# Spilled and kept rows of a branchformer backward kernel: 128-partition transfers in place of 112 and 13, with a new instruction order

## The chip, the cores and the metric

The kernel runs on one core of a Trainium2 chip. The metric is device time in microseconds (us) of one execution; three runs of the kernel before gave 1150.36, 1152.78 and 1153.01 us, so its median is 1152.78 us. Less is better.

## What is computed

Forward and all gradients of one branchformer block, for two batches of 4000 tokens of 144 channels, in bfloat16. Cut to what matters:

```python
B, T, D, K = 2, 4000, 144, 5
xa = layernorm(x)
q, k, v = split(xa @ w_qkv)
p = softmax(q @ k.T * D ** -0.5)            # 4000 x 4000 for each batch
glob = (p @ v) @ w_att_out
u, g = split(gelu(xa @ w_mlp_in)); g = layernorm(g)
gc = sum_i shift(g, i) * dw_csgu[i]         # 5 taps over tokens
loc = (u * gc) @ w_mlp_out
m = concat(glob, loc); m = m + sum_i shift(m, i) * dw_merge[i]
out = x + m @ w_merge
# returned: out, and the gradients of out against x and the seven weights, for grad_out
```

## The kernel before

**Tiles and stages.** The 4000 tokens of a batch stand as 125 partitions of 32 tokens (`PB` = 125, `NB` = 32). So every token tile has 125 rows. The kernel has three stages. The *head* loads x, grad_out and the weights, normalises x and multiplies weight matrices together. The *attention loop* then runs over 64 row blocks (32 of each batch), some 15 us each. The *end* multiplies the outputs and the gradients of the weights.

**The attention loop.** For row block `i` TensorE writes scores and, one step later, the gradient of the probabilities into PSUM (`ps`, two buffers, in runs of eight matmuls; the lines of `quad`). VectorE reads each piece of scores with L1209, which puts the negative into `Pbuf` and keeps its minimum; ScalarE makes exponentials of it in place (L1215) and copies the other half out of PSUM (L1225); VectorE multiplies (L1226). Each half of a row block of `Pbuf` and `Sbuf` is then turned by a transposing DMA on SyncE's queue into `PT` and `ST` (L1219, L1405), and TensorE multiplies those by xa (`yz`, L1236 and L1266) and adds up `X` (L1322), which VectorE adds to `acc` (L1329). `qb` and `dhr` go through transposing DMAs too.

**Beside it** the local branch (`local_units`) runs for pairs of token blocks, in steps 2 to 26 for batch 0 and again for batch 1. Its 16 pairs are visited starting with the last one, because the five taps reach over block borders; what the last pair left in the ring tiles `hgr` (u and the gate), `dugr` and `gpr` (gate values) goes out to DRAM tiles `keep` when it is made (`e_gp`) and comes back into slot 0 near the end (`e_hold`). `held` does the same for two pairs of the taps' ring.

**Spills.** There is no room for both batches, so batch 0's normalised x (`xa_aug`) goes to `xa_d` in eight pieces (`spill_xa0`) and its sums (`acc`, f32) to `acc_d` in four (`spill_acc0`); in the end stage `load_xa0` and `load_acc0` bring them back into `xa0r` and `acc0`.

**How 125 rows travel.** Each such transfer is made by `move` as two DMAs, one of partitions 0 to 111 and one of the last 13 (L47 and L48). `Yn_d`, `Zn_d` and `ug_d` already have 128 rows and go in one DMA each.

**What sets the order.** Each engine's instructions are first written in program order. `Planner.plan` then cuts them into runs (up to 8 or 16 matmuls on TensorE, one instruction elsewhere) and chains the runs of each engine in the order that a table of numbers, `Planner.ORDER`, gives. SyncE's DMAs are one such list, GpSimd's instructions another. An engine takes its instructions strictly in this order, so a DMA whose input is late holds up every DMA behind it on SyncE's queue.

Of the kernel before, what the change touches and what calls it, by code (L numbers as in the profile page):

```python
# [8 lines left out]
BF = mybir.dt.bfloat16  # L9
# [514 lines left out]
def local_units(k, W, b, S, A, es, DHT, ps_w, gw):  # L524
# [11 lines left out]
    keep = [tc.dram_tile([PB, G2, n], BF, name="keep%d_%d" % (b, i)) for i, n in enumerate((D, D, 2 * D))]  # L536
# [12 lines left out]
    hgr = mk("hgr", [PB, G2, 2 * D], 3)  # L549
    dugr = mk("dugr", [PB, G2, D], 3)  # L550
    gpr = mk("gpr", [PB, G2, 2 * D], 3)
# [79 lines left out]
    def e_hold():  # L631
        for i in range(2):
            move(nc.sync, ring[:, :, 8 + 2 * i:10 + 2 * i, :], held[i])
        move(nc.sync, hgr[0][:, :, 0:D], keep[0][:])
        move(nc.sync, dugr[0][:], keep[1][:])
        move(nc.sync, gpr[0][:], keep[2][:])
# [5 lines left out]
    def e_gp(g):  # L642
        nc.vector.tensor_tensor(sq[:], z_[:], a_[:], op=ALU.mult)
        nc.vector.tensor_tensor(gpr[new(g)][:], sq[:], q_[:], op=ALU.add)
        if g == NG2 - 1:
            move(nc.sync, keep[0][:], hgr[new(g)][:, :, 0:D])
            move(nc.sync, keep[1][:], dugr[new(g)][:])
            move(nc.sync, keep[2][:], gpr[new(g)][:])
# [127 lines left out]
class Planner:  # L776

    ORDER = {
# [759 lines left out]
class Merge:  # L1538
# [81 lines left out]
    def open_late(self):  # L1620
# [16 lines left out]
        self.Zn = [None, None]  # L1637
        m0 = self.pool(self.es_m0, "mrg_m0", 1, "left")
        S = self.SS[0]
        S.acc = m0.tile([PB, NB, D], F32, name="acc0")  # L1640
        S.xa_aug = m0.tile([PB, NB, XW], BF, name="xa0r")

    def load_xa0(self):
        k, S = self.k, self.SS[0]
        for g in range(2):
            sl = slice(16 * g, 16 * g + 16)
            move(k.nc.sync, S.xa_aug[:, sl, 0:D], k.xa_d[:, sl, :])
# [545 lines left out]
```

## Time and profile before

| what | value |
|---|---|
| median of 3 runs | 1152.78 us (1150.36 to 1153.01) |
| the profiled execution's own time | 1152.39 us |
| its span, first to last instruction | 1150.5 us |
| TensorE busy | 1118.8 us, 97% |
| VectorE busy | 1021.0 us, 89% |
| ScalarE busy | 906.5 us, 79% |
| GpSimd busy | 249.5 us, 22% |
| SyncE's DMA queue, share of 16 DMA engines' span | 84.6% |

The own time is 1.9 us more than the span: what lies around the first and last instruction. TensorE's busy time is modelled from pipelined matmuls, so a busy TensorE isn't TensorE at its peak. A row of waits names the instruction that waited, what ended the wait, the total in us, the number of waits and the longest. PE is TensorE, PEld its weight loads, DVE VectorE, ACT ScalarE, POOL GpSimd, SP SyncE; a q behind a name is that engine's own queue of issues.

### The profile page before, as it was taken

The numbers are of one execution on the slowest core, as the hardware profiler recorded it, in microseconds if no ns is written. First come the engines' busy times: TensorE is split into PE (matmuls) and PEld (weight loads), VectorE is DVE, ScalarE is ACT, GpSimd is POOL, SyncE is SP. The second block draws the span as 40 slices with busy tenths as digits, with TensorE's granted clock in tenths as the row PEclk, the third lists the DMA queues.
The fourth block names the chain that finished last, engine by engine and source line by source line (L and its number), as shares of the span: only waits on it lengthen the run. The fifth ranks groups of instructions, "written<-read, shape, count | busy, mean of one in ns | idle before, by whom it ended". The sixth has DMA issues, their size and how long they took to land.

```text
span 1150.5 us, 35851 instructions
## 1 busy us (share of the span) xinstructions
PE 1118.8 (97%) x14293; PEld 868.7 (76%) x14293; DVE 1021.0 (89%) x3063; ACT 906.5 (79%) x1641; POOL 249.5 (22%) x427
## 2 busy tenths in 40 slices
PE   6999999999999999999999999999999999999998
PEld 3667777777777677777777777777777777699987
DVE  8699999999999998877999999999999997667656
ACT  5999898899898767777989889888889877615372
POOL 8111112111121113431001111111111112013642
PEclk9999999999999999999999999999999999999999
DMA  4688887979988989998988989888888899978973
GB/s 117 155 160 176 173 181 158 192 159 173 174 166 159 188 181 182 201 187 183 207 183 178 171 158 168 161 181 152 173 174 154 187 177 183 224 173 219 245 144 101
DMA packets 680887, 200.72 MB, mean 174 GB/s; under 512 B 657815, under 2 KB 674093, under 8 KB 680699
## 3 DMA queue, kind: packets, MB, share of 16 engines
q1 hardware_dynamic: 678352, 194.69, 84.6%
q0 software_dynamic: 2192, 3.62, 1.1%
q8 instruction: 111, 1.82, 0.7%
q14 instruction: 56, 0.46, 0.1%
q10 hardware_dynamic: 176, 0.12, 0.0%
HBM read 24.62 MB, written 18.01 MB: 37 GB/s over the span
## 4 chain that ended last, share of the span: by engine, by line
PE 64%; DMA 13%; DVE 11%; ACT 7%; issue 2%; SPq 1%; POOL 1%; ACTq 0%; DVEq 0%; POOLq 0%
PE X L1322 18%; PE ps L1187 14%; PE yz L1236 8%; PE yz L1266 8%; PE ps L1194 5%; DMA PT<-Pbuf 5%; DVE Pbuf L1209 4%; ACT Pbuf L1215 3%; PE po L1708 2%; DMA ST<-Sbuf 2%; PE pd L610 1%; DVE Sbuf L1226 1%; PE pj L1147 1%; ACT Sbuf L1225 1%; DMA go_h<-in_grad_out_dram 1%
## 5 line engine op out<-in xcount | busy, mean ns | idle before, releaser
L1209 DVE TENSOR_SCALAR_CACHE_REDUCE Pbuf<-ps 125x1000 bf16<-125x1000 f32 x256 | 306.2, 1197 | 30.1 <-PE ps L1194 22.4
L1225 ACT CAST Sbuf<-ps 125x1000 bf16<-125x1000 f32 x249 | 248.7, 999 | 86.7 <-PE ps L1194 66.2
L1215 ACT ACTIVATE Pbuf<-Pbuf,nm 125x1000 bf16<-125x1000 bf16 x256 | 284.9, 1144 | 4.4 <-DVE nm L1211 4.2
L1322 PE MATMUL X<-QBs,Pbuf 125*128 125x144 bf16 x2048 | 281.1, 226 | 0.2 <-POOL QBs L1256 0.2
L1322 PE MATMUL X<-QBs,Sbuf 125*128 125x144 bf16 x2048 | 281.3, 226 | 0.0
L1187 PE MATMUL ps<-xaT_m,qt 128*128 128x500 bf16 x1024 | 260.6, 374 | 5.0 <-DVE Pbuf L1209 3.5
L1322 PEld LDWEIGHTS <-Sbuf 125*128 125x128 bf16 x2048 | 198.2, 98 | 18.8 <-issue 18.5
L1322 PEld LDWEIGHTS <-Pbuf 125*128 125x128 bf16 x2048 | 200.2, 98 | 1.3 <-issue 1.1
L1226 DVE TENSOR_TENSOR Sbuf<-Sbuf,Pbuf 125x1024 bf16<-125x1024 bf16 x249 | 170.8, 690 | 7.9 <-ACT Sbuf L1225 6.0
L1236 PE MATMUL yz<-xa_aug,PT 125*128 125x145 bf16 x2048 | 151.0, 227 | 6.5 <-DMA PT<-Pbuf 6.4
L1266 PE MATMUL yz<-xa_aug,ST 125*128 125x144 bf16 x2048 | 150.8, 228 | 3.6 <-DMA ST<-Sbuf 2.4
L1236 PEld LDWEIGHTS <-PT 125*128 125x128 bf16 x2048 | 130.7, 98 | 21.6 <-DMA PT<-Pbuf 10.5
L1187 PEld LDWEIGHTS <-qt 128*128 128x128 bf16 x1024 | 91.4, 97 | 68.6 <-issue 7.0
L1266 PEld LDWEIGHTS <-ST 125*128 125x128 bf16 x2048 | 132.9, 98 | 12.2 <-issue 7.1
L1329 DVE TENSOR_TENSOR acc<-X,acc 125x432 f32<-125x432 f32 (+1 forms) x204 | 109.8, 548 | 15.3 <-PE X L1322 14.8
L1256 POOL TENSOR_TENSOR QBs<-g,g 125x144 bf16<-125x144 f32 x64 | 35.2, 550 | 379.2 <-ACT g L1255 290.9
L1194 PEld LDWEIGHTS <-qt 16*128 16x128 bf16 x1024 | 26.3, 91 | 108.9 <-issue 108.9
L1194 PE MATMUL ps<-XR,qt 16*128 16x500 bf16 x1016 | 100.4, 380 | 0.0
L681 POOL TENSOR_SCALAR l_w<-ring,nc,c 125x144 f32<-125x144 bf16 x64 | 31.8, 504 | 167.0 <-DVE nc L677 122.4
L653 DVE TENSOR_TENSOR l_prod<-ring,Wc 125x720 bf16<-125x720 bf16 x128 | 65.9, 535 | 0.2
L1611 PE MATMUL Hps<-Yg,go_h 125*128 125x144 bf16 x640 | 54.3, 226 | 0.0
L600 POOL TENSOR_TENSOR rsr<-ve,mhalf 125x2 f32<-125x2 f32 x32 | 25.4, 795 | 126.9 <-DVE ve L599 107.4
(540 smaller groups left out, 1946.4 us busy)
## 6 DMA issues: line engine op xcount, KB each, us to landing
Yn_d<-yn SPq DMA_DIRECT2D x64, 36.0 KB
Zn_d<-qb SPq DMA_DIRECT2D x64, 36.0 KB
ug_d<-ugr SPq DMA_DIRECT2D x32, 72.0 KB
Yg<-Yn_d SPq DMA_DIRECT2D x8, 288.0 KB
Yg<-ug_d SPq DMA_DIRECT2D x8, 288.0 KB
Zn<-Zn_d SPq DMA_DIRECT2D x4, 576.0 KB
PT<-Pbuf SPq DMA_TRANSPOSE x128
ST<-Sbuf SPq DMA_TRANSPOSE x128
```

Of the source, the lines that this page charges most:

```text
L653: nc.vector.tensor_tensor(prod[:, bi].rearrange("p a b -> p (a b)"), ring[:, a, p + bi:p + bi + 5, :].rearrange("p a b -> p (a b)"), W.Wc[ ...
L1187: mm = nc.tensor.matmul(pp[r // 2][:, r % 2, 0:CH], QT[i][:, 2 * h, :], bs(i)[0].xaT_m[:, c * CH:(c + 1) * CH], start=True, stop=False)
L1194: nc.tensor.matmul(pp[r // 2][:, r % 2, 0:CH], QT[i][rs, 2 * h + 1, :], xr, start=False, stop=True)
L1209: nc.vector.tensor_scalar(pv(pc(i, c2)), src, -1.0, 3.0e38, op0=ALU.mult, op1=ALU.min, accum_out=NM[i][:, c2:c2 + 1])
L1215: nc.scalar.activation(v, v, ACT.Exp, bias=NM[i][:, 4:5], scale=-1.0)
L1225: nc.scalar.copy(pv(sc(i, c2)), src)
L1226: nc.vector.tensor_tensor(sc(i, c2), sc(i, c2), pc(i, c2), op=ALU.mult)
L1236: nc.tensor.matmul(Yw, PT[0:PB, pos(i, j), :], S.xa_aug[:, j, 0:D + 1], start=(j == 0), stop=(j == NB - 1))
L1266: nc.tensor.matmul(Zw, ST[0:PB, j, :], S.xa_aug[:, j, 0:D], start=(j == 0), stop=(j == NB - 1))
L1322: nc.tensor.matmul(X[:, jj, :], l, r, start=(n_ == 0), stop=(n_ == len(ops) - 1))
L1329: nc.vector.tensor_tensor(av, X[0:PB, 0:nj, :], av, op=ALU.add)
L1611: nc.tensor.matmul(H[0:rows, a // 3, (a % 3) * D:(a % 3 + 1) * D], lhs, self.src[b][h][:, 2 + j, :], start=(n == 0 and a % 3 == 0), stop=( ...
```

## The change

The tiles `hgr`, `dugr`, `gpr`, `acc`, `xa_aug`, `acc0` and `xa0r` and the DRAM tiles `keep`, `acc_d` and `xa_d` get 128 rows; compute uses views of the first 125. Thirty pairs of DMAs become thirty DMAs of 128 partitions: twelve of `keep` (three out and three back in each batch), eight to `xa_d`, four to `acc_d`, four from it and two from `xa_d`. The three rows that nobody writes are cleared: `acc` and the ring buffers by GpSimd memsets (one of 32 x 4608 f32, three small ones in each batch), `xa_aug` by two DMAs of zeros. `held` still goes as 112 and 13. SyncE's list goes from 826 to 798 instructions, GpSimd's from 423 to 430, and all five lists of `ORDER` are new.

```diff
-    keep = [tc.dram_tile([PB, G2, n], BF, name="keep%d_%d" % (b, i)) for i, n in enumerate((D, D, 2 * D))]
+    keep = [tc.dram_tile([128, G2, n], BF, name="keep%d_%d" % (b, i)) for i, n in enumerate((D, D, 2 * D))]
-    hgr = mk("hgr", [PB, G2, 2 * D], 3)
-    dugr = mk("dugr", [PB, G2, D], 3)
-    gpr = mk("gpr", [PB, G2, 2 * D], 3)
+    def whole(name, n):
+        full = mk(name, [128, G2, n], 3)
+        nc.gpsimd.memset(full[2][96:128], 0.0)
+        return full, [t[0:PB] for t in full]
+    hgf, hgr = whole("hgr", 2 * D)
+    dugf, dugr = whole("dugr", D)
+    gpf, gpr = whole("gpr", 2 * D)
...
-        move(nc.sync, hgr[0][:, :, 0:D], keep[0][:])
+        nc.sync.dma_start(hgf[0][:, :, 0:D], keep[0][:])
...
-            move(nc.sync, keep[0][:], hgr[new(g)][:, :, 0:D])
+            nc.sync.dma_start(keep[0][:], hgf[new(g)][:, :, 0:D])
...
     ORDER = {
-        "PE": [36, 37, 38, 39, 40, 41, 0, 1, 42, 2, 3, 4, 5, 43, ...
+        "PE": [36, 37, 38, 39, 40, 41, 0, 42, 1, 2, 3, 4, 5, 6, 43, ...
...
-            move(k.nc.sync, S.xa_aug[:, sl, 0:D], k.xa_d[:, sl, :])
+            k.nc.sync.dma_start(self.xa0[:, sl, 0:D], k.xa_d[:, sl, :])
...
-            move(k.nc.sync, S.acc[:, sl, :], k.acc_d[:, sl, :])
+            k.nc.sync.dma_start(self.acc0[:, sl, :], k.acc_d[:, sl, :])
...
-    k.spill_xa0 = lambda j: move(nc.sync, k.xa_d[:, j:j + 4, :], SS[0].xa_aug[:, j:j + 4, 0:D])
-    k.spill_acc0 = lambda sl: move(nc.sync, k.acc_d[:, sl, :], acc[:, sl, :])
+    k.spill_xa0 = lambda j: nc.sync.dma_start(k.xa_d[:, j:j + 4, :], SS[0].xa_full[:, j:j + 4, 0:D])
+    k.spill_acc0 = lambda sl: nc.sync.dma_start(k.acc_d[:, sl, :], accf[:, sl, :])
...
     def clear_a():
+        nc.gpsimd.memset(accf[96:128], 0.0)
+        for a, n in ((0, 25), (25, 7)):
+            nc.sync.dma_start(SS[0].xa_full[PB:128, a:a + n, :].rearrange("p a b -> p (a b)"), k.zdram[0:128 - PB, 0:n * XW])
```

SyncE's queue where the program begins, before. `Sbuf<-in_x_dram` are the loads of x, `raw` the weights, `dwt` the merge taps, which TensorE turns at L215:

```order
L42 DMA Sbuf<-in_x_dram 112x1152
L2020 DMA zdram<-zt 128x128
L43 DMA Sbuf<-in_x_dram 13x1152
L42 DMA Sbuf<-in_x_dram 112x1152
L154 DMA raw<-in_w_att_out_dram 16x144
L154 DMA raw<-in_w_merge_dram 16x144
L42 DMA go_q_95<-in_grad_out_dram 112x1152
L1118 DMA Sbuf<-zdram 3x4096
L157 DMA dwt<-in_dw_merge_dram 5x288
```

The same queue from its first DMA, after:

```order
L42 DMA Sbuf<-in_x_dram 112x1152
L43 DMA Sbuf<-in_x_dram 13x1152 x3
L157 DMA dwt<-in_dw_merge_dram 5x288
L42 DMA Sbuf<-in_x_dram 112x1152
L153 DMA raw<-in_w_mlp_out_dram 128x144
L2026 DMA zdram<-zt 128x128
L153 DMA raw<-in_w_merge_dram 128x144
```

The load of `dwt` went from the fourteenth DMA of the queue to the fifth.

SyncE's queue where the kept rows of batch 0 come back, before. `PT` and `ST` are the transposes that TensorE waits for:

```order
L48 DMA ring<-held_0_923 13x2x288
L1405 DMA_TRANSPOSE ST<-Sbuf 128x16x128
L1248 DMA Yn_d_69<-yn_133 128x144
L1219 DMA_TRANSPOSE PT<-Pbuf 128x16x128 x2
L48 DMA hgr_934<-keep_0_926 13x2x144
L1165 DMA_TRANSPOSE qt<-qb_128 128x6x128
L691 DMA_TRANSPOSE dhT<-dhr_948 128x6x128
L48 DMA dugr_937<-keep_1_927 13x288
```

The same place, after (the lines of the same statements are 4 higher):

```order
L1409 DMA_TRANSPOSE ST<-Sbuf 128x16x128
L639 DMA dugr_941<-keep_1_930 128x288
L1252 DMA Yn_d_69<-yn_132 128x144
L1409 DMA_TRANSPOSE ST<-Sbuf 128x16x128
L1223 DMA_TRANSPOSE PT<-Pbuf 128x16x128 x2
L48 DMA ring<-held_1_927 13x2x288
L640 DMA gpr_945<-keep_2_931 128x576
L638 DMA hgr_937<-keep_0_929 128x2x144
```

Three returns of one DMA each stand where six stood, later in the row of transposes and closer together.

GpSimd's queue ahead of the first `QBs` (which `X` needs), before:

```order
L402 COPY go_r_96<-go_q_95 125x608
L548 MEMSET ugr_931 32x288
L2023 MEMSET A_dWiT 128x432
L1256 TENSOR_TENSOR QBs<-g_910,g_911 125x144
L1256 TENSOR_TENSOR QBs<-g_1190,g_1191 125x144
```

and after:

```order
L402 COPY go_r_96<-go_q_95 125x608
L282 TENSOR_TENSOR sr_806<-two,cols 128x80 x2
L282 TENSOR_TENSOR sr_834<-two,cols 128x80
L2029 MEMSET acc 32x4608
L1136 MEMSET yn_133 32x144
L1260 TENSOR_TENSOR QBs<-g_913,g_914 125x144
```

The new memset of `acc` stands two rows ahead of the first `QBs`.

On TensorE the two orders are nearly one: of 1385 runs, 785 stand at the same place in both, and none moved by more than 12. On VectorE 464 of 2521 stand at the same place, and half moved by two or less.

More of the change, by code (lines that the diff above doesn't have):

```diff
@@ L633, in e_hold @@
             move(nc.sync, ring[:, :, 8 + 2 * i:10 + 2 * i, :], held[i])
-        move(nc.sync, hgr[0][:, :, 0:D], keep[0][:])
-        move(nc.sync, dugr[0][:], keep[1][:])
-        move(nc.sync, gpr[0][:], keep[2][:])
+        nc.sync.dma_start(hgf[0][:, :, 0:D], keep[0][:])
+        nc.sync.dma_start(dugf[0][:], keep[1][:])
+        nc.sync.dma_start(gpf[0][:], keep[2][:])
     def e_m(g):
@@ L645, in e_gp @@
         if g == NG2 - 1:
-            move(nc.sync, keep[0][:], hgr[new(g)][:, :, 0:D])
-            move(nc.sync, keep[1][:], dugr[new(g)][:])
-            move(nc.sync, keep[2][:], gpr[new(g)][:])
+            nc.sync.dma_start(keep[0][:], hgf[new(g)][:, :, 0:D])
+            nc.sync.dma_start(keep[1][:], dugf[new(g)][:])
+            nc.sync.dma_start(keep[2][:], gpf[new(g)][:])
     def taps(g, a):
@@ L778 @@
     ORDER = {
[53 rows of a table removed]
-        "DVE": [0, 2, 1, 3, 4, 10, 5, 11, 9, 8, 6, 7, 12, 14, 15, 13, 16, 17, 40, 43, 25, 18, 44, 20, 22, 23, 19, 32, 24, 21, 34, 33, 35, 36, 26, 28,
[99 rows of a table removed]
[53 rows of a table added]
+        "DVE": [0, 2, 3, 1, 4, 9, 11, 8, 5, 6, 7, 10, 12, 14, 15, 16, 17, 21, 13, 18, 23, 25, 22, 19, 20, 24, 32, 44, 34, 40, 33, 35, 36, 41, 26, 43,
[99 rows of a table added]
             2476, 2477, 2478, 2479, 2480, 2456, 2428, 2486, 2485, 2481, 2482, 2483, 2487, 2430, 2484, 2488, 2462, 2491, 2489, 2429, 2427, 2492, 2490,
@@ L934 @@
             2509, 2517, 2510, 2511, 2512, 2518, 2519, 2520],
-        "Activation": [1, 0, 4, 5, 2, 3, 7, 6, 8, 9, 10, 13, 29, 32, 14, 15, 11, 33, 16, 17, 18, 12, 37, 35, 34, 19, 20, 21, 24, 22, 23, 31, 27, 26,
[64 rows of a table removed]
-        "Pool": [8, 5, 15, 4, 11, 0, 12, 10, 1, 3, 47, 7, 2, 16, 18, 6, 19, 17, 41, 25, 26, 24, 50, 33, 32, 31, 9, 53, 37, 38, 20, 30, 42, 23, 13,
[44 rows of a table removed]
+        "Activation": [0, 1, 2, 4, 3, 5, 8, 10, 9, 11, 7, 29, 6, 13, 14, 12, 15, 32, 38, 16, 18, 31, 17, 37, 30, 35, 19, 23, 24, 20, 21, 27, 26, 22,
[64 rows of a table added]
+        "Pool": [2, 7, 0, 5, 6, 47, 8, 15, 4, 11, 9, 1, 12, 16, 18, 19, 10, 41, 17, 26, 25, 24, 32, 33, 31, 37, 50, 3, 38, 20, 35, 42, 34, 30, 22,
[44 rows of a table added]
     }
@@ L1639, in open_late @@
         S = self.SS[0]
-        S.acc = m0.tile([PB, NB, D], F32, name="acc0")
-        S.xa_aug = m0.tile([PB, NB, XW], BF, name="xa0r")
+        self.acc0, self.xa0 = m0.tile([128, NB, D], F32, name="acc0"), m0.tile([128, NB, XW], BF, name="xa0r")
+        S.acc, S.xa_aug = self.acc0[0:PB], self.xa0[0:PB]
     def load_xa0(self):
@@ L1970 @@
     bx = pool(ctx, "bx", "left")
-    acc = bx.tile([PB, NB, D], F32, name="acc")
+    accf = bx.tile([128, NB, D], F32, name="acc")
+    acc = accf[0:PB]
     rstd = [bx.tile([PB, NB], F32, name="rstd_x%d" % b) for b in range(B)]
@@ L1979 @@
             setattr(S, nm + "_d", tc.dram_tile([128, NB, D], BF, name="%s_d%d" % (nm, b)))
-    k.acc_d = tc.dram_tile([PB, NB, D], F32, name="acc_d")
-    k.xa_d = tc.dram_tile([PB, NB, D], BF, name="xa_d")
+    k.acc_d = tc.dram_tile([128, NB, D], F32, name="acc_d")
+    k.xa_d = tc.dram_tile([128, NB, D], BF, name="xa_d")
     def open_batch(b, side):
@@ L1985, in open_batch @@
         px = pool(es_x[b], "xa%d" % b, side)
-        S.xa_aug = px.tile([PB, NB, XW], BF, name="xa_aug%d" % b)
+        S.xa_full = px.tile([128, NB, XW], BF, name="xa_aug%d" % b)
+        S.xa_aug = S.xa_full[0:PB]
         pa = pool(es_x[b], "bt%d" % b, side)
```

516 rows, old and new, of the table ORDER are left out of this document.

## The prediction

> **What bounds the kernel now.** I read the page first: its span and its busy times.
>
> ```profile
> span 1150.5 us, 35851 instructions
> PE 1118.8 (97%) x14293; PEld 868.7 (76%) x14293; DVE 1021.0 (89%) x3063; ACT 906.5 (79%) x1641; POOL 249.5 (22%) x427
> ```
>
> TensorE leaves 31.7 us of the span idle. Nothing that only moves transfers can win more than this. The table by stretches of 50 us then says where the other engines stand (columns: stretch, its length, busy time with count of PE, PEld, DVE, ACT and POOL, granted clock, DMA share, GB/s).
>
> ```profile
> 200.00:250.00 50.00, 50.00 (x638) 38.30 (x637) 49.11 (x147) 45.77 (x80) 9.27 (x16) 1.00 0.84 168
> 400.00:450.00 50.00, 46.47 (x601) 34.64 (x599) 45.02 (x139) 32.18 (x54) 11.47 (x19) 1.00 0.93 184
> ```
>
> In a steady stretch of the attention loop TensorE is busy all 50.00 us and VectorE 49.11; the clock is 1.00. Both engines are full there, and neither number changes with the way in which a spill travels. Where batch 0's local branch ends (second row), TensorE has 3.5 us idle. So the question is which of TensorE's waits are for DMAs. The waits of TensorE, and those of its weight loads, in which a late transpose shows first:
>
> ```profile
> PE hps L170 <- DMA raw<-in_w_qkv_dram: 6.3, 1, 6.3
> PE ps L1187 <- DVE Pbuf L1209: 3.5, 12, 0.9
> ...
> PEld L1236 <- DMA PT<-Pbuf: 10.5, 18, 1.3
> PEld L1266 <- DMA ST<-Sbuf: 4.2, 7, 1.5
> PEld L1187 <- DMA qt<-qb: 1.5, 3, 0.7
> ```
>
> The weight loads wait 10.5 + 4.2 + 1.5 = 16.2 us for transposes in the whole program. None of these waits names a kept or spilled row. Such a row can only cost time by standing ahead of a transpose on SyncE's queue, or by taking the DMA engines from it. The same view by the stretches in which kept and spilled rows travel densest, in order 73 to 97 (first row), 364 to 420 (three rows) and 530 to 605 us (two rows):
>
> ```profile
> PEld L1266 <- DMA ST<-Sbuf: 1.0, 1, 1.0
> ...
> PEld L1236 <- DMA PT<-Pbuf: 2.6, 4, 1.1
> PEld L1187 <- DMA qt<-qb: 0.6, 1, 0.6
> PEld L1266 <- DMA ST<-Sbuf: 0.5, 2, 0.3
> ...
> PEld L1236 <- DMA PT<-Pbuf: 1.3, 1, 1.3
> PEld L1266 <- DMA ST<-Sbuf: 0.3, 1, 0.3
> ```
>
> Together 6.3 us in 10 waits. This is the most that the transfers themselves can give back.
>
> **The change part by part.** *Thirty issues fewer.* The issues of 13 rows on SyncE's queue, from the answers on the tiles `keep`, `acc_d` and `xa_d` (durations in ns, least/median/most):
>
> ```profile
> L48 SPq DMA_DIRECT2D keep<-hgr x2: 842/890/938, 79.9 to 583.1; - x2
> L48 SPq DMA_DIRECT2D keep<-dugr x2: 543/546/550, 88.9 to 574.0; - x2
> L48 SPq DMA_DIRECT2D keep<-gpr x2: 427/480/534, 94.7 to 597.5; - x2
> L48 SPq DMA_DIRECT2D hgr<-keep x2: 863/865/867, 378.7 to 908.2; - x2
> L48 SPq DMA_DIRECT2D dugr<-keep x2: 343/415/487, 383.5 to 901.0; - x2
> L48 SPq DMA_DIRECT2D gpr<-keep x2: 389/467/545, 412.3 to 925.3; - x2
> ...
> L48 SPq DMA_DIRECT2D acc_d<-acc x4: 338/460/1199, 536.1 to 589.0; - x4
> L48 SPq DMA_DIRECT2D acc<-acc_d x4: 327/399/403, 1032.9 to 1053.3; - x4
> ...
> L48 SPq DMA_DIRECT2D xa_d<-xa_aug x8: 369/520/547, 27.4 to 510.5; - x8
> L48 SPq DMA_DIRECT2D xa0r<-xa_d x2: 408/980/1553, 1047.2 to 1064.4; - x2
> ```
>
> By medians: `keep` 2 x (0.890 + 0.546 + 0.480 + 0.865 + 0.415 + 0.467) = 7.3 us, `acc_d` 4 x 0.460 + 4 x 0.399 = 3.4, `xa_d` 8 x 0.520 + 2 x 0.980 = 6.1. That is 16.9 us of queue time in 30 issues, 0.56 each, in a span of 1150. All of it is hidden except where a transpose right behind is late. Of the 10 waits I can't say from the trace which has a removed issue ahead of it. If each had one, each would shrink by at most 0.56, and by no more than it is long: below 10 x 0.56 = 5.6 us. The longest of the second stretch (1.1) has none:
>
> ```profile
> 376.85 6.34 DMA PT<-Pbuf
> ...
> 383.23 1.20 PE yz L1236 x16
> ...
> 375.18 3.45 SPq L1219 DMA_TRANSPOSE PT<-Pbuf  x2
> 378.72 0.87 SPq L48 DMA_DIRECT2D hgr<-keep  x1
> ```
>
> Here (the chain, then SyncE's timeline) both transposes were issued ahead of the kept row, and the second took 6.34 us until TensorE could start; what it lost, it lost on the DMA engines. There the change takes no bytes away: 128 rows for 125 are 2.4% more. So I take two fifths of the 6.3 us: **-2.5 us**, between 0 and -5.6.
>
> The Trainium skill (*DMA: Bandwidth & Descriptors*, Rules for kernel authors) says of two transfers to disjoint partition halves that they serialize on the same engines, and to use one of 128 partitions; and that under 64 KB one pays mostly overhead. By that rule the pieces of 13 rows are nearly pure cost, all 5.6 us would come back, and the sum would be 1146.4; the trace agrees that a small piece is no cheaper to issue, and shows no one who waits for it.
>
> *The last rows back in the end stage.* `acc0` has a waiter, on VectorE:
>
> ```profile
>   DVE dx_s L1720: 1.2, 1
> ...
> 1050.00:1100.00 50.00, 49.55 (x805) 49.17 (x802) 36.75 (x165) 20.52 (x39) 31.00 (x52) 1.00 1.00 236
> ```
>
> VectorE has 13 us free in that stretch and TensorE is full, so this 1.2 us costs nothing, and its going gives nothing: 0.
>
> *Clearing.* The memset of 32 x 4608 f32 isn't in the trace. The nearest f32 one:
>
> ```profile
> L2023 POOL MEMSET A_dWiT<- 128x432 f32 x1 | 0.5, 462 | 0.1
> ...
> 42.07 0.33 POOL L548 MEMSET ugr<- 32x288 bf16 x1 [11.26 <-PE pt L350]
> 42.46 0.46 POOL L2023 MEMSET A_dWiT<- 128x432 f32 x1
> 49.48 0.74 POOL L1256 TENSOR_TENSOR QBs<-g,g 125x144 bf16<-125x144 f32 x1 [6.55 <-ACT g L1254]
> ```
>
> 462 ns for 432 elements of a row is 1.07 ns each, so 4608 take some 4.9 us as an estimate. It stands between `go_r` and the first `QBs`, where GpSimd idles 11.26 + 6.55 us. Cost 0; with that cover gone, up to 4.9. The six small ones (288 to 576 elements) are at most 0.6 us each, on an engine that is 22% busy: 0. The two DMAs of zeros go behind the loads of the head, where no transpose is due yet: 0, at worst two issues, 1.1 us.
>
> *The new order at the beginning.* TensorE's transposes of `dwt` waited 1.41 us, since its load was issued as the fourteenth DMA, at 7.43:
>
> ```profile
> 7.43 3.08 DMA dwt<-in_dw_merge_dram
> ...
> 10.56 0.50 PE L215 MATMUL hps<-ident,dwt 5*128 5x5 bf16 x4 [1.41 <-DMA dwt<-in_dw_merge_dram]
> 10.99 0.81 PE L392 MATMUL pt<-ident,xa_aug 125*128 125x125 bf16 x6
> ...
> 9.53 1.05 DVE L385 TENSOR_SCALAR xa_aug<-Sbuf,rstd_x,lnnm 125x144 bf16<-125x144 bf16 x4
> ```
>
> Now it is the fifth, and can land before TensorE gets there. Late next is `xa_aug`: VectorE ends it at 10.58, so L392 starts there instead of 10.99: **-0.4 us**, between 0 and -1.4.
>
> *The new order elsewhere.* TensorE's runs stand almost where they stood (785 of 1385 at the same place), so its distances to what it waits for are the same within a run or two: 0. VectorE's order changed at four places in five, by mostly one or two places; with 49.11 of 50 us busy it has no room, and this can go either way. I bound it with the two rivals on the order.
>
> **The sum.** -2.5 - 0.4 = -2.9 us. The profiled execution took 1152.39 (span 1150.5 and 1.9 around it): 1149.5. That execution lies 0.4 us below the median of 1152.78, so against the median the forecast is -0.28%. A measurement of this kernel can tell about 0.3%, 3.5 us, from no change: faster means below 1149.3, slower above 1156.2. The forecast lies just inside the first border.
>
> **The rivals.**
>
> *Nothing returns.* All of the removed issues were hidden; the late transposes are late through the DMA engines (as at 376.85). For it: no compute engine waits for a `keep` or for `xa_d`. Against it: 10 waits fall where these rows travel. Time: 1152.4, or 1152.0 with the head. The Trainium skill (*DMA: Bandwidth & Descriptors*, Rules for kernel authors) advises to issue a DMA early and wait late, since the fixed cost then overlaps; by that rule this rival holds, and the trace agrees for all of them but the 1.2 us on `acc`.
>
> *Slower: VectorE frees the score buffers later.* PSUM holds two buffers `ps`; TensorE's next scores wait until L1209 has read the last ones. Now this happens 12 times for 3.5 us, 0.29 each, in 256 reads. If the new order puts another VectorE instruction ahead of the read often enough to make it 36 times, this adds 24 x 0.29 = 7.0 us: 1149.5 + 7.0 = 1156.5, and 1159.4 without the gain of 2.9. It decides from 10 more such waits on, which eat up the gain. For it: 49.11 of 50 us. Against it: small moves, and TensorE's row beside them the same.
>
> *Much faster: the order also clears other waits.* Of the 31.7 us idle, 6.3 + 1.4 are the first loads, and the last 50 us hold 4.75:
>
> ```profile
> 1100.00:1150.00 50.00, 45.25 (x676) 40.36 (x673) 31.01 (x133) 25.40 (x71) 16.96 (x23) 0.99 0.48 115
> ```
>
> About 19 us are left in the loop. Half of it gone gives 1152.4 - 9.5 = 1142.9. For it: the order was made anew with fewer DMAs. Against it: so few runs of TensorE moved.
>
> **How the numbers follow.** The forecast with its near surroundings (1146 to 1152) 0.50: of it 0.27 faster, 0.23 the same. Nothing returns 0.14: 0.13 the same, 0.01 slower. Slower by the buffers, or by the memset losing its cover, 0.23. Much faster 0.13. That makes faster 0.40, same 0.36, slower 0.24. The likeliest case is the forecast, 1149.5, its own range 1146 to 1152. The range for 8 in 10 reaches into both order rivals: down to 1142.5, below which I leave about half of the much faster case (0.07), and up to 1159.5, the slower case without the gain, above which 0.09 stay.
>
> **What would show it.** Right: weight loads' waits for `PT`, `ST` and `qt` near 13.7 us instead of 16.2, with the loss between 364 and 420 us; no wait of L215; first `QBs` near 49 us; waits of L1187 for L1209 near 3.5. Wrong: waits for transposes as before (nothing returns), waits of L1187 for L1209 above 7 us (buffers), TensorE's idle time below 22 us (much faster), or a wait of VectorE's first `acc` for the memset.

## The result, and the profile after

The changed kernel takes **1163.64 us** (median of six runs, 1159.32 to 1169.28); the kernel before takes 1151.56 us beside it. The ratio is 1.011, its 95% interval 1.0075 to 1.0145. So the change makes the kernel slower by about 12 us. The forecast was 1149.5, and its range ended at 1159.5.

The page of the profiled execution (own time 1164.37 us), its span and busy times:

```profile
span 1162.6 us, 35807 instructions
PE 1121.7 (96%) x14293; PEld 870.8 (75%) x14293; DVE 1016.5 (87%) x3063; ACT 906.8 (78%) x1641; POOL 255.8 (22%) x434
```

TensorE now leaves 1162.6 - 1121.7 = 40.9 us idle where it left 31.7, which is 9.2 more, and it is busy 2.9 us longer. The waits after (who waited, for whom, us in all, times, longest):

```profile
PEld L1240 <- DMA PT<-Pbuf: 13.3, 19, 1.6
...
PEld L1270 <- DMA ST<-Sbuf: 8.6, 13, 1.8
...
PE ps L1191 <- DVE Pbuf L1213: 4.1, 15, 0.9
...
PEld L1191 <- DMA qt<-qb: 3.2, 4, 1.4
...
PE pt L392 <- ACT cols L218: 2.5, 1, 2.5
...
PE fpt L1765 <- DVE R L1793: 2.1, 1, 2.1
```

The weight loads wait 13.3 + 8.6 + 3.2 = 25.1 us for transposes, where it was 16.2 before and where I forecast 13.7. The score buffers, my rival on the slow side, wait 4.1 us in 15 waits (3.5 in 12 before): they aren't it. Two new waits stand at the ends: L392 in the head and L1765 in the end stage. They don't carry the loss: e11 below has both (2.7 and 2.3 us) and isn't slower than the kernel before.

The stretches of 50 us in which TensorE was short (the first columns after the length are TensorE's busy time and count):

```profile
200.00:250.00 50.00, 49.60 (x632) 38.16 (x628) 48.87 (x149) 44.57 (x81) 9.49 (x16) 1.00 0.88 172
...
400.00:450.00 50.00, 44.03 (x559) 32.10 (x558) 42.14 (x130) 30.98 (x52) 9.38 (x16) 1.00 0.99 181
450.00:500.00 50.00, 47.95 (x606) 36.64 (x603) 41.79 (x128) 36.47 (x55) 19.98 (x39) 1.00 0.91 178
```

The steady stretch lost 0.4 us; the stretch from 400, where batch 0's local branch ends and the kept rows return, lost 46.47 - 44.03 = 2.4. The stretch from 450 was this before:

```profile
450.00:500.00 50.00, 49.89 (x635) 38.20 (x633) 42.92 (x129) 39.98 (x63) 23.11 (x48) 1.00 0.98 189
```

It lost 49.89 - 47.95 = 1.9. Together that is 4.4 of the 9.2 us.

### The profile page after: what moved, and what is told of

Its sections match the earlier page's. It is cut to its first block, busy times and chain, and to the rows that moved or that the text cites. A ratio compares the mean times of both kernels' runs of the same rounds, so it can differ in the third digit from the quotient of the medians.

```text
span 1162.6 us, 35807 instructions
## 1 busy us (share of the span) xinstructions
PE 1121.7 (96%) x14293; PEld 870.8 (75%) x14293; DVE 1016.5 (87%) x3063; ACT 906.8 (78%) x1641; POOL 255.8 (22%) x434
## 4 chain that ended last, share of the span: by engine, by line
PE 68%; DVE 11%; DMA 9%; ACT 8%; issue 2%; POOL 1%; SPq 0%; ACTq 0%; DVEq 0%; POOLq 0%
PE X L1326 18%; PE ps L1191 13%; PE yz L1240 9%; PE yz L1270 8%; DMA PT<-Pbuf 6%; PE ps L1198 5%; DVE Pbuf L1213 4%; PE po L1712 3%; ACT Pbuf L1219 3%; PE Hps L1615 2%; DMA ST<-Sbuf 2%; ACT Sbuf L1229 2%; DVE Sbuf L1230 1%; PE pd L614 1%; PE pj L1151 1%
## 5 line engine op out<-in xcount | busy, mean ns | idle before, releaser
L1326 PEld LDWEIGHTS <-Sbuf 125*128 125x128 bf16 x2048 | 198.3, 98 | 19.0 <-issue 18.7
L1240 PE MATMUL yz<-xa_aug,PT 125*128 125x145 bf16 x2048 | 150.8, 227 | 9.1 <-DMA PT<-Pbuf 7.6
L1240 PEld LDWEIGHTS <-PT 125*128 125x128 bf16 x2048 | 130.5, 98 | 25.3 <-DMA PT<-Pbuf 13.3
L1270 PEld LDWEIGHTS <-ST 125*128 125x128 bf16 x2048 | 132.6, 98 | 16.7 <-DMA ST<-Sbuf 8.6
L1739 ACT ACTIVATE t<-t,dx_c,rstd_x 125x144 f32<-125x144 f32 x64 | 28.7, 500 | 35.7 <-DVE t L1738 22.7
```

Source lines behind the costliest of these rows:

```text
L1240: nc.tensor.matmul(Yw, PT[0:PB, pos(i, j), :], S.xa_aug[:, j, 0:D + 1], start=(j == 0), stop=(j == NB - 1))
L1270: nc.tensor.matmul(Zw, ST[0:PB, j, :], S.xa_aug[:, j, 0:D], start=(j == 0), stop=(j == NB - 1))
L1326: nc.tensor.matmul(X[:, jj, :], l, r, start=(n_ == 0), stop=(n_ == len(ops) - 1))
```

## The experiments

The change has two parts that can be taken apart: the transfers (with the clearing) and the order. Below, "old" and "new" order mean the five lists of before and of the changed kernel. The first two kernels make the other two of a two by two table. A list of numbers says nothing to a reader, so the diffs show which list stands where.

| kernel | us | ratio to before (95%) | loads' waits for PT + ST + qt |
|---|---|---|---|
| before: old transfers, old order | 1151.56 | 1 | 16.2 |
| after: new, new | 1163.64 | 1.011 (1.0075 to 1.0145) | 25.1 |
| e1: old transfers, new order | 1171.58 | 1.0169 (1.0143 to 1.0195) | 23.9 |
| e2: new transfers, old order | 1148.92 | 0.9974 (0.9959 to 0.9990) | 12.7 |
| e3: e2, new order up to row block 14 | 1147.60 | 0.9967 (0.9955 to 0.9980) | 10.3 |
| e4: e2, new order from 14 to 40 | 1161.53 | 1.0084 (1.0069 to 1.0098) | 17.4 |
| e5: e2, new order from 40 on | 1150.59 | 0.9989 (0.9976 to 1.0002) | 11.7 |
| e6: after, 20 moves in SyncE's list | 1179.77 | 1.0219 (1.0186 to 1.0251) | 18.7 |
| e7: e2, new order from 22 to 31 | 1153.49 | 1.0026 (1.0013 to 1.0039) | 13.6 |
| e8: of e7, SyncE and GpSimd alone | 1158.34 | 1.0073 (1.0055 to 1.0091) | 16.7 |
| e9: of e7, TensorE alone | 1157.72 | 1.0071 (1.0054 to 1.0088) | 6.9 |
| e10: of e7, VectorE and ScalarE alone | 1158.15 | 1.0076 (1.0060 to 1.0092) | 7.6 |
| e11: after, old order from 14 to 40 | 1147.69 | 0.9980 (0.9963 to 0.9997) | 11.0 |
| e12: after, 11 moves in SyncE's list | 1160.98 | 1.0094 (1.0076 to 1.0112) | 16.2 |

**Transfers or order: e1 and e2.**

```diff
 # e1: the kernel before
-    ORDER = old
+    ORDER = new, with the 112 and 13 where the new list has the one of 128
 # e2: the changed kernel
-    ORDER = new
+    ORDER = old, with the one of 128 where the old list has the 112;
+            memset of acc behind go_r, the ring's behind those of ugr, zeros behind sWr_d
```

> The kernel before (transfers of 112 and 13 rows, no clearing) with the changed kernel's order on all five engines; where one DMA of 128 rows stands there, the two pieces stand here, one behind the other. If the new order costs the time (theory: order), 1159 to 1169 us, as the changed kernel. If the transfers of 128 rows or the clearing cost it (theory: transfers), 1150 to 1154, as the kernel before. If the thirty saved issues do help as predicted but the order takes more, 1 to 4 us above the changed kernel's 1163.6.

> The changed kernel's transfers and clearing with the order of the kernel before; each DMA of 128 rows stands where its piece of 112 rows stood, and the added clearing stands in gaps of GpSimd's and SyncE's queues at the beginning. Theory order: 1147 to 1153 us, at or below the kernel before, and the predicted 1149.5 if two fifths of the transposes' waits go. Theory transfers: 1159 to 1168. If the transfers change nothing by themselves: 1151 to 1153.

Measured: 1171.58 us (ratio 1.0169, 1.0143 to 1.0195) and 1148.92 us (ratio 0.9974, 0.9959 to 0.9990); before beside them 1151.85. So the transfers of 128 partitions, put where the old ones were, gain 2.9 us (1.2 to 4.7 by the interval). The new order loses 1.7% with the old transfers and some 1.4% with the new ones. The waits of e2's weight loads:

```profile
PEld L1262 <- DMA PT<-Pbuf: 8.1, 15, 1.4
...
PEld L1292 <- DMA ST<-Sbuf: 2.4, 3, 1.4
PEld L1213 <- DMA qt<-qb: 2.2, 4, 1.1
```

12.7 us in all: 3.5 less than before, which is the size of the gain. (In the rows of e2 and of all later kernels the statements of the attention loop stand 22 lines lower than in the changed one: L1262 is L1240 there.) In the three stretches in which kept and spilled rows travel densest, e2 has these left (none from 73 to 97, two rows from 364 to 420, two from 530 to 605):

```profile
PEld L1262 <- DMA PT<-Pbuf: 1.0, 2, 0.8
PEld L1213 <- DMA qt<-qb: 0.5, 1, 0.5
...
PEld L1262 <- DMA PT<-Pbuf: 0.3, 1, 0.3
PEld L1292 <- DMA ST<-Sbuf: 0.2, 1, 0.2
```

That is 2.0 us where the kernel before had 6.3; in the rest of the program it is 10.7 for 9.9. So the waits went where the forecast said that they would.

**Where along the program: e3, e4, e5 and e11.** From the start of each row block's scores in the traces of the changed kernel and of e2, which run the same program in two orders, the changed kernel was 0.4 us behind at row block 14, 12 at row block 40 and 14.7 at the end. So I joined the orders at the beginning of row blocks.

```diff
 # e3
+    ORDER = new[: row block 14] + old[row block 14 :]
 # e4
+    ORDER = old[: 14] + new[14 : 40] + old[40 :]
 # e5
+    ORDER = old[: 40] + new[40 :]
 # e11
+    ORDER = new[: 14] + old[14 : 40] + new[40 :]
```

> The program with the new transfers; the new order up to the first scores of row block 14, the old order behind it. The step starts of the two full orders (new transfers in both) lie 0.4 us apart at row block 14, 12 us apart at row block 40 and 14.7 us at the end. Theory 'late places' (the new order costs time where single transposes come late, mostly between row blocks 22 and 40): 1148.9 + 0.5 = 1149.4 us. Rival 'even pace' (the new order makes each row block a little longer, 14.7/62 = 0.24 us each): 1148.9 + 12 x 0.24 + 0.6 of the head = 1152.4 us.

> New transfers; old order up to row block 14, the new order from there to row block 40, the old one behind. 'Late places': most of the loss, 11 to 12 us: 1160 us, and the weight loads' waits for PT, ST and qt near 21 us where the old order has 12.7 and the new one 25.1. 'Even pace': 26 x 0.24 = 6.2: 1155.1 us.

> New transfers; old order up to row block 40, the new one from there to the end. 'Late places': 14.7 - 12 = 2.7: 1151.6 us. 'Even pace': 24 x 0.24 = 5.8: 1154.7 us. If e3, e4 and e5 together lose much less than 14.7 us, the loss needs the orders of more than one part at once.

> The changed kernel (new transfers, new order) with the old order in one stretch alone, from the first scores of row block 14 to those of row block 40, on all engines: the other half of e4. If the stretch holds the loss, it returns here: the changed kernel's 1163.6 less e4's 11 to 12.6, or the sum of what e3 (-1.3) and e5 (+1.7) showed against 1148.9: 1149 to 1152 us. If the loss came from anything in the new order that works all along the program, 1156 us or more.

Measured: 1147.60, 1161.53, 1150.59 and 1147.69 us. Against e2's ratio of 0.9974, e4 loses 0.0110, or 12.7 us; e5 loses 0.0015, 1.7 us, which its interval doesn't separate from nothing; e3 loses nothing. "Even pace" falls (it asked for 1155.1 in e4). e11 is the other half of the proof: with the old order in that one stretch the changed kernel goes from 1.011 to 0.998. Within these intervals the whole loss is made between row blocks 14 and 40. The expectation of e4 on the weight loads' waits failed, though: 17.4 us where 21 were expected. Others came beside them, of TensorE for the first load of grad_out of batch 1 and for sums:

```profile
PE pt L477 <- DMA pgo_h<-in_grad_out_dram: 3.1, 1, 3.1
PE X L1348 <- DVE acc L1355: 2.0, 1, 2.0
```

**Why these transposes are late: e6 and e12.** At the largest such wait of the changed kernel, SyncE's timeline (start, duration, instruction) and TensorE's:

```profile
405.13 1.21 SPq L1169 DMA_TRANSPOSE qt<-qb  x1
406.40 1.63 SPq L639 DMA_DIRECT2D dugr<-keep  x1
408.08 0.41 SPq L1252 DMA_DIRECT2D Yn_d<-yn  x1
408.60 1.60 SPq L1409 DMA_TRANSPOSE ST<-Sbuf  x1
...
412.58 1.19 PE L1270 MATMUL yz<-xa_aug,ST 125*128 125x144 bf16 x16 [1.60 <-DMA ST<-Sbuf]
```

Four issues stand back to back, a kept row among them, and TensorE waits 1.60 us for the last. The theory "queue" said: put such small transfers behind the transpose.

```diff
 # SyncE's list, one of e6's eight places (also one of e12's four)
     qt<-qb
-    dugr<-keep
-    Yn_d<-yn
     ST<-Sbuf    # row block 23, second half
+    dugr<-keep
+    Yn_d<-yn
```

> The changed kernel with twenty moves in SyncE's list alone, at eight places where TensorE waited for a transpose in its profile: the small transfers that stood ahead of a transpose of PT or ST (dugr, keep, ring, held, Zn_d, Yn_d, ug_d, acc_d, xa_d, and at two places a transpose of qt or dhT that nobody wants yet) now stand right behind it. The order of the other engines stays the new one. Theory 'queue' (these transposes are late because SyncE issues other transfers first: 0.9 to 2.9 us at ST of row blocks 23 and 35, PT of 28, 15 and 57; or because the transfers just ahead make its own issue twice as long): the stalls at these places (1.8, 1.2, 2.5, 1.1, 1.0, 0.6, 0.9, 1.6; 10.7 in all) go for the most part; with half of it coming back later as other waits, 5 us are left: 1158.5 us where the changed kernel has 1163.6. Rival 'producers' (ScalarE and VectorE finish Pbuf and Sbuf later in the new order, and the queue only hides that): within 1.5 us of the changed kernel, 1162 to 1164 us.

> The changed kernel with eleven moves in SyncE's list, at four places only: the small transfers ahead of ST of row blocks 23 and 35 and of PT of 15 and 57 stand right behind these transposes. None of the moved transfers is one for which TensorE or VectorE was seen to wait in e6 (there the moves behind PT of 23 and 28, ST of 32 and 59 made new waits). In the profile of the changed kernel the transposes were issued 0.9, 2.9, 1.1 and 1.8 us after their data were ready, and TensorE waited 1.8, 1.2, 1.1 and 1.0 us. Theory 'queue at these places': 0.9 + 1.2 + 1.1 + 1.0 = 4.2 us at most, with half of it made up for elsewhere 2 us: 1161.5 us. Theory 'fit' (any single list that is moved alone makes new waits somewhere): 1163 us or more.

(The times "after their data were ready" in both texts count from the last write into the buffer ahead of the issue, whichever rows it wrote; so they are lower bounds.) Measured: e6 **1179.77 us** (ratio 1.0219), 16 us slower than the kernel it was to mend (13 by the ratios). I had missed this entirely. The waits of e6:

```profile
PEld L1292 <- DMA ST<-Sbuf: 7.9, 7, 5.0
...
PE pt L477 <- DMA gq<-in_grad_out_dram: 3.6, 1, 3.6
```

and the waits of the same profile between 555 and 570 us:

```profile
DVE acc L1353 <- DMA acc_d<-acc: 3.7, 1, 3.7
...
PE ph L580 <- DVE acc L1353: 3.4, 1, 3.4
```

The spill of `acc` that I had put behind a transpose has a waiter: VectorE may not write the next sums into `acc` until the spill has read it; TensorE's next products wait for that. The load of `gq` has a waiter on TensorE too. The longest wait, 5.0 us for `ST`, is for a transpose that landed 11.98 us after its issue (last section); that the moves caused it isn't shown. The granted clock of TensorE is lower too: 0.990 to 0.995 in e6's six executions, 0.995 to 0.999 in those of the changed kernel, and e6's two shortest (1171.07 and 1172.31 us) are the two with the highest clock. e12 keeps four of the eight places, those with no such waiter: 1160.98 us, ratio 1.0094 (1.0076 to 1.0112), which is what "queue" expected (1161.5), but its ratio gives 1162.4 beside the changed kernel's 1163.64, and the two intervals overlap. So the queue can be part of it, and this doesn't settle how much.

**One engine's list at a time: e7 to e10.** Between row blocks 22 and 31 the lists can be exchanged one by one.

```diff
 # in e2, from row block 22 to 31
 # e7
+    all five lists: new
 # e8
+    SyncE, GpSimd: new      TensorE, VectorE, ScalarE: old
 # e9
+    TensorE: new            the others: old
 # e10
+    VectorE, ScalarE: new   the others: old
```

> The program with the new transfers; the old order everywhere but from the first scores of row block 22 to those of row block 31, where all five engines have the new one. In the profiles the new order loses 7.5 us between row blocks 22 and 30, the kernel with the new order from 14 to 40 the same 7.4. Old order in full: 1148.9 us. Expected 1148.9 + 7.5 = 1156.4 us, by every theory; if it is below 1152, the loss in this stretch needs what came before it.

> As before, but in that stretch only SyncE's and GpSimd's lists have the new order; TensorE, VectorE and ScalarE keep the old. Theory 'queue' (transposes and loads of the next batch are late because of where they stand among SyncE's transfers): most of the 7.5 us, 1154 us or more, with waits of TensorE's weight loads for PT, ST and qt above 16 us. Theory 'producers': 1149 to 1150 us. Theory 'fit' (no engine's list is bad by itself; a list is fitted to the others, and a change of one alone makes new waits): each of the three parts costs as much as all of them together or more, 1155 us or more here.

> As before, but in that stretch only TensorE's list has the new order (28 of its 1385 runs stand elsewhere among the others). Theory 'TensorE asks earlier': most of the 7.5 us, 1154 us or more. Theories 'queue' and 'producers': 1149 to 1150 us. 'Fit': 1152 us or more, less than the other two since so few runs moved.

> As before, but in that stretch only VectorE's and ScalarE's lists have the new order (155 and 62 instructions stand elsewhere among the others). Theory 'producers' (Pbuf, Sbuf and qb are finished later): 1154 us or more, with the transposes of row blocks 23 to 28 issued later by 1 to 2 us against the scores they come from. Theory 'queue': 1149 to 1150 us. 'Fit': 1155 us or more.

Measured against e2's ratio: all five lists cost 0.0052, 6.0 us; SyncE's and GpSimd's alone 0.0099, 11.4; TensorE's alone 0.0097, 11.2; VectorE's and ScalarE's alone 0.0102, 11.7. (The kernel before took 1149.51 us beside these four, so e7's 1153.49 would be 1155.8 beside e2's 1151.85; 1156.4 was expected.) Each part alone costs about twice what all together cost, and e7's interval lies below those of the other three. "Queue" and "producers" each expected two of these three kernels at 1149 to 1150 us; none is there. "TensorE asks earlier" got its price in e9, but says nothing of e8 and e10. "Fit" stands: what a list costs depends on the other four. It doesn't say why the five new lists together cost 6.0 us here; that stays open. It missed one point: TensorE's list, with the fewest moves, costs as much as the others. What waits, depends on which list was changed. In e8, TensorE's waits between 350 and 510 us:

```profile
PE yz L1292 <- DMA ST<-Sbuf: 5.4, 2, 3.9
PE pt L477 <- DMA gq<-in_grad_out_dram: 2.9, 1, 2.9
```

In e9, the same stretch:

```profile
PE pj L1169 <- DVE acc L1355: 2.6, 2, 1.6
PE ps L1213 <- DVE Pbuf L1235: 2.0, 5, 0.6
PE X L1348 <- DVE acc L1355: 1.5, 1, 1.5
```

and in e10:

```profile
PE yz L1262 <- DVE qb L1296: 6.1, 1, 6.1
```

Changed transfers make TensorE wait for transfers, a changed TensorE makes it wait for VectorE's sums, changed vector work for vector work. Behind the 6.1 us of e10 there is a transfer all the same. VectorE writes `qb` at 468.53, after this instruction of batch 1, which had itself waited for a load of x:

```profile
467.19 0.31 DVE L455 BATCH_NORM_STATS2 pst<-xa_aug 125x6 f32<-125x144 bf16 x1 [5.12 <-DMA xa_aug<-in_x_dram]
```

SyncE issued that load at 464.05, and in e2 at 463.99; but in e2 VectorE had written this `qb` at 460.89 and came to its next such instruction at 467.77. So the new list of VectorE put an instruction of the next batch ahead of `qb`, and the old list of SyncE brings its input later than that. (e9's profiled execution was its shortest, 1154.24 us, so its rows show only a part of the 11.2.) In e9 and e10 the weight loads wait only 6.9 and 7.6 us for transposes, less than in e2, and both are 11 us slower than e2.

## Why the prediction was wrong

*Thirty issues fewer, -2.5 us: right.* Alone (e2) the transfers gave 2.9 us (interval of the ratio 0.9959 to 0.9990), and the waits for transposes went to 12.7 us for 13.7 forecast. With the new order the same transfers seem to be worth more (1.0169 in e1, 1.011 after, some 7 us, intervals that just touch); why, I don't know. So "nothing returns" is out, if narrowly. The place was right too (6.3 us of waits became 2.0 where these rows travel). That two fifths of 6.3 came so near the gain is partly luck: the share was a choice between nothing and all.

*Rows back in the end stage: as forecast, but not tried alone.* VectorE's wait for `acc` at L1720 (1.2 us, and 0.3 more at L1723) is 1.0 us in e2 and gone in the changed kernel.

*Clearing: right.* The memset of `acc` and the first `QBs`:

```profile
L2029 POOL MEMSET acc<- 32x4608 f32 x1 | 3.9, 3935 | 0.1
...
47.44 0.49 POOL L1260 TENSOR_TENSOR QBs<-g,g 125x144 bf16<-125x144 f32 x1 [11.41 <-DMA sWr_d<-sWr]
```

3.9 us where I estimated 4.9, and `QBs` isn't later (47.44; 49.48 before). No instruction waits for the memset.

*The new order at the beginning, -0.4 us: the size came, by another cause, and didn't stay.* TensorE's rows in the head after:

```profile
7.49 0.49 PE L215 MATMUL hps<-ident,dwt 5*128 5x5 bf16 x4
10.51 0.27 PE L392 MATMUL pt<-ident,xa_aug 125*128 125x125 bf16 x1 [2.53 <-ACT cols L218]
11.89 0.92 PE L392 MATMUL pt<-ident,xa_aug 125*128 125x125 bf16 x7 [1.12 <-DVE xa_aug L385]
```

L215 no longer waits and runs 3.1 us earlier, L392 starts 10.99 - 10.51 = 0.48 earlier; then it waits once more for the next `xa_aug`. What let L392 start was ScalarE's `cols`, which I had not seen, and not the end of `xa_aug` at 10.58; so the 0.48 for 0.4 is luck. At row block 14 nothing of it is left (229.5 us in e3, 229.6 in e2), and e3 and e2 can't be told apart by their times.

***The new order elsewhere: 0.* This is the step that failed.** It measured +12.7 us between row blocks 14 and 40 (e4), and ahead of and behind it -0.8 and +1.7 (e3, e5), neither told from nothing. Its reason, that TensorE's runs stand almost where they stood and so its distances to what it waits for are the same, has two faults. The new place of 28 runs among nine row blocks, with the other four lists old, costs 11.2 us (e9): the number of runs that moved says nothing about the price. And the distance to a producer is set by both lists: with TensorE's list left as it was, the other lists alone cost 11.4 and 11.7 (e8, e10). I had bounded this step by the rivals, and the slow one took a single mechanism, the score buffers, at most 7.0 us. The buffers' waits rose by 0.6 us. Most of the loss sits in waits for transposes instead. From the first scores of row block 14 to those of row block 40 (229.99 to 638.57 us in the changed kernel, 229.62 to 626.44 in e2, 11.8 less), TensorE itself waits for them as follows in the changed kernel:

```profile
PE yz L1270 <- DMA ST<-Sbuf: 4.9, 6, 1.6
PE yz L1240 <- DMA PT<-Pbuf: 3.6, 7, 0.8
...
PE ps L1191 <- DMA qt<-qb: 1.3, 1, 1.3
```

and in e2:

```profile
PE yz L1292 <- DMA ST<-Sbuf: 1.7, 2, 1.1
...
PE yz L1262 <- DMA PT<-Pbuf: 1.0, 2, 0.6
```

That is 9.8 us against 2.7, so 7.1 of the 11.8. About half of the idle time that TensorE gained falls between 400 and 500 us, in part where it already had 3.5 us idle before: I had read that row as room for a gain, and it may as well mark a place where the lists are tight. Why the new lists let these transposes come late stays open: e12, which moved transfers at four places, doesn't settle the queue's part, and e8 to e10 show only that no single list carries the loss.

The sum by the runs: -2.9 for the transfers, about +15 for the order, so +12.

## What to carry to other kernels

A change that comes with new instruction orders is two changes; build the one without the other first. Here the edit alone won 0.26% and the orders with it lost 1.4%. A new order can't be costed at nothing because few instructions moved: in a kernel that is 97% full on one engine, what late inputs cost was not won back later (12 us behind at row block 40, 14.7 at the end). Before a transfer is put behind another in a queue, look up who waits for what it reads as well as for what it writes (e6's spill of `acc`). The version to keep is e2 or e3 (0.9967, 0.9955 to 0.9980), which beat both kernels.

## What the runs showed of the hardware that I had not expected

A wait of TensorE can cost more than itself, since the granted clock falls behind it. e10 after its 6.1 us (columns as above; the number behind GpSimd's is the granted clock):

```profile
460.00:464.00 4.00, 2.44 (x26) 1.43 (x24) 2.08 (x7) 1.29 (x3) 1.51 (x4) 1.00 1.12 255
464.00:468.00 4.00, 0.00 (x0) 0.00 (x0) 0.81 (x3) 0.78 (x1) 0.00 (x0) 0.71 0.45 105
468.00:472.00 4.00, 3.06 (x27) 3.06 (x27) 3.46 (x12) 1.13 (x1) 0.00 (x0) 0.50 0.03 7
472.00:476.00 4.00, 4.00 (x50) 3.13 (x49) 2.58 (x12) 2.24 (x5) 1.45 (x4) 0.94 1.06 129
```

In the changed kernel, the 1.60 us shown at 412.58 (first row) and the 2.1 us of L1765:

```profile
412.00:416.00 4.00, 3.42 (x42) 2.56 (x43) 3.13 (x17) 0.99 (x1) 0.00 (x0) 1.00 1.15 246
...
1120.00:1124.00 4.00, 3.91 (x34) 3.60 (x34) 2.39 (x10) 2.40 (x5) 1.08 (x3) 0.57 1.02 245
```

After L1765's wait TensorE ran 4 us at 0.57, which is 4 x 0.43 = 1.7 us of its work at full clock; after the 1.60 the clock stayed at 1.00. The length of the wait doesn't decide it alone. In e7 a wait of 1.9 us for `ST` ends at 411.64 and one of 2.0 us for grad_out at 443.55:

```profile
412.00:416.00 4.00, 4.00 (x31) 2.63 (x30) 2.19 (x10) 0.36 (x1) 0.00 (x0) 0.64 0.93 212
...
444.00:448.00 4.00, 4.00 (x55) 3.13 (x53) 2.56 (x10) 2.41 (x5) 0.00 (x0) 1.00 1.17 199
```

The clock fell behind the shorter one alone. The Trainium skill (*TensorE: Matmul & The Clock Gate*, Part 1: The HAM clock gate) says that the clock falls to half after an idle window of about 3.4 us, and that the windows run freely. The half agrees with the 0.50 of e10; the length doesn't, since here waits of 2.1 and 1.9 us met it already. The lower clock may explain part of why TensorE's *busy* time grew from e2's 1117.4 to 1121.7 us: the mean granted clock was 1.000 in e2's profile and 0.998 in that of the changed kernel, which by an estimate (0.002 of 1162.6 us) is some 2 of the 4 us. It doesn't always show in the time: e4 took 1160.62 us at 0.994 and 1161.43 at 0.998.

A transpose can take far longer than usual. In e6 the issues of `PT` (least/median/most in ns), and one of them:

```profile
L1245 SPq DMA_TRANSPOSE PT<-Pbuf x128: 1557/1832/8238, 31.3 to 1034.9; - x128
...
992.95 8.24 SPq L1245 DMA_TRANSPOSE PT<-Pbuf  x1
```

It stands behind the first loads of the end stage. The transpose that TensorE waited 5.0 us for was issued ahead of it and of those loads (the second of two issues, at 988.24), and it landed while the 8.24 us ran:

```profile
986.54 3.57 SPq L1431 DMA_TRANSPOSE ST<-Sbuf  x2
...
988.24 11.98 DMA ST<-Sbuf
```

What made both so long wasn't tried.
